# A 2-D FFT filter refactored: 32-point row DFT first, folded column DFTs, no spectrum transposes

## The chip, the cores and the metric

The kernel runs on one core of a Trainium2 chip. The metric is the device time of one execution in microseconds, as the median of several runs; lower is better. The profile's own clock (its "span") leaves out some 1.5 to 2 us at the ends. Engines are named as in the profile: PE is TensorE, PEld its weight load, DVE is VectorE, ACT is ScalarE, POOL is GpSimd, SP issues transfers. "Ratio" always means the mean time of one kernel's fast runs over the mean of the other's fast runs of the same rounds, so it is not quite the ratio of the medians quoted beside it.

## The reference, cut to what matters

```python
def reference(A_x, A_w_r, A_w_i, B_x, B_w_gate, B_w_up, B_w_down):
    xn = _layernorm(A_x, axis=-1)                       # [1, 2048, 640], bf16 in
    # filter: 2-D real FFT, product with a complex table, inverse
    X  = rfft2(xn.astype(float32), axes=(-2, -1)) * (A_w_r + 1j * A_w_i)
    a  = irfft2(X, s=(2048, 640), axes=(-2, -1)).astype(bfloat16)
    # gated bilinear unit, hidden size 1536
    b  = ((xn @ B_w_gate) * (xn @ B_w_up)) @ B_w_down
    return A_x + a + b                                  # bf16
```

(`rfft2` and `irfft2` are written in full in the reference; B_x is not used.) Both branches end up as matmuls: the transforms are products with tables of cosines and sines.

## The kernel before

A small scheduler inside the kernel plans every instruction at build time, from estimated durations, and fixes the order on each engine; on the chip each engine runs its list in that order and waits on semaphores. TensorE interleaves the filter's small matmuls with the gate and up projection ("GU", ten matmuls of 256 columns a tile, 96 tiles) and the down projection.

The filter before: each block of 128 rows is transposed, goes through the DFT over the 640 features (which has the even and odd features apart), is folded while it is read from PSUM, and goes through a 128-point DFT. Then the spectrum is transposed, goes through 16-point DFTs, is multiplied by the filter, and comes back the same way. Two parts:

```python
# fold of the feature DFT: each addition has one operand in PSUM (e3), one in SBUF (v_osb)
e3 = ps[:, bk, 0:324].rearrange("p (c l) -> p c l", c=2)
c.e.tensor_tensor(v_a[:, ar, :, 0:161], e3[:, :, 0:161], v_osb[:, ar, :, 0:161], AluOpType.add)
c.e.tensor_tensor(v_a[:, ar, 0, 320:160:-1], e3[:, 0, 0:160], v_osb[:, ar, 0, 0:160], AluOpType.subtract)
c.e.tensor_tensor(v_a[:, ar, 1, 320:160:-1], v_osb[:, ar, 1, 0:160], e3[:, 1, 0:160], AluOpType.subtract)
# ...
# layer norm of blocks 2 to 15: two passes on GpSimd, x - m and then * rs
c.e.tensor_scalar(v_xn[:, sl, :], v_x[:, slx, :], 1.0, v_nmbf[:, b:b + 1], AluOpType.mult, AluOpType.add)
c.e.tensor_scalar(v_xn[:, sl, :], v_xn[:, sl, :], v_rs[:, b:b + 1], 0.0, AluOpType.mult, AluOpType.add)
```

## Time and profile before

| | before |
|---|---|
| time, median of the first 3 runs | 239.8 us (239.51 to 242.7) |
| span of the profiled run | 238.3 us |
| TensorE busy | 232.5 us, 98% |
| VectorE busy | 173.8 us, 73% |
| GpSimd busy | 24.3 us, 10% |

The prediction below shows the lines on busy time, clock and chain. Three more views. First the slices of the page (40 equal slices of 6 us; each digit is the busy share in tenths):

```profile
PE   8979999999999999999999999999999999999995
...
DVE  5969998855479999999847422222278888888895
...
POOL 0027856800000000000000000000000000000000
```

TensorE shows 9 from the fourth slice to the last but one. GpSimd works in slices 3 to 8 only, about 12 to 48 us: that is the layer norm of the later blocks. Second, the lines of the page on GpSimd's two passes and on the largest fold (operands, count, then busy us and mean ns of one, then the idle time before them):

```profile
L797 POOL TENSOR_SCALAR arena<-arena 128x640 bf16<-128x640 bf16 x14 | 11.0, 798 | 17.0 <-DVE arena L742 14.9
...
L808 POOL TENSOR_SCALAR arena<-arena 128x640 bf16<-128x640 bf16 x14 | 11.1, 807 | 6.1 <-DVE arena L786 6.1
...
L865 DVE TENSOR_TENSOR arena<-ps,arena 128x322 bf16<-128x322 f32 x16 | 7.8, 488 | 3.6 <-ACT arena L856 3.5
```

A fold reads `ps,arena`: one operand from PSUM, one from SBUF (`ps` is the kernel's buffer in PSUM, which the matmuls write, `arena` its one large buffer in SBUF). Third, what TensorE waited for in the first 62 us (us in total, times, longest):

```profile
PE ps L879 <- DMA arena<-c_t: 1.8, 1, 1.8
PE ps L700 <- DVE arena L707: 1.1, 1, 1.1
```

### The profile page before, as it was taken

Reading aid. Unit: us, or ns where it says so; the run is one execution under the profiler, and the core shown is the slowest. Engines: PE = TensorE matmul, PEld = TensorE weight load, DVE = VectorE, ACT = ScalarE, POOL = GpSimd, SP = SyncE. Lnnn points to the kernel's source line nnn. Section 1 sums busy time; section 2 is a strip of 40 time slices with the busy share of each in tenths; the row PEclk is TensorE's granted clock in tenths of the full one; section 3 lists DMA queues with packets and bytes.
Section 4 is the critical chain, followed back from the end, with each engine's and each line's share of the span. In section 5 each row is a group of like instructions: output and inputs, shape, how many; then the busy total and the mean of one; then the engine's idle time right before and its main releaser. Section 6 shows DMA issues by size and latency. Waiting matters only on the chain.

```text
span 238.3 us, 5579 instructions
## 1 busy us (share of the span) xinstructions
PE 232.5 (98%) x2274; PEld 197.8 (83%) x2274; DVE 173.8 (73%) x502; ACT 108.9 (46%) x181; POOL 24.3 (10%) x35
## 2 busy tenths in 40 slices
PE   8979999999999999999999999999999999999995
PEld 8968888787999999998988888888787787787773
DVE  5969998855479999999847422222278888888895
ACT  2135667676554565554577555555223223223120
POOL 0027856800000000000000000000000000000000
PEclk9999999999999999999999999999999999999999
DMA  6999700960720000001072100000013223123221
GB/s 199 346 338 384 260 3 0 256 190 0 267 89 3 3 0 3 0 3 56 3 241 92 55 3 0 0 3 0 17 43 98 56 69 99 55 73 96 68 60 55
DMA packets 18953, 21.35 MB, mean 90 GB/s; under 512 B 1520, under 2 KB 17520, under 8 KB 18800
## 3 DMA queue, kind: packets, MB, share of 16 engines
q1 hardware_dynamic: 18928, 20.99, 27.7%
q8 instruction: 18, 0.29, 0.5%
q14 instruction: 7, 0.06, 0.1%
HBM read 18.37 MB, written 2.62 MB: 88 GB/s over the span
## 4 chain that ended last, share of the span: by engine, by line
PE 93%; SPq 3%; DMA 2%; DVE 1%; issue 0%; ACT 0%
PE ps L1064 44%; PE ps L1211 22%; PE ps L846 5%; SPq L666 3%; PE ps L1112 3%; DMA arena<-c_t 2%; PE ps L1159 2%; PE ps L977 2%; PE ps L1158 2%; PE ps L998 2%; PE ps L921 2%; PE ps L942 2%; PE ps L821 2%; PE ps L1122 2%; PE ps L879 1%; PE ps L880 1%
## 5 line engine op out<-in xcount | busy, mean ns | idle before, releaser
L1064 PE MATMUL ps<-arena 128*128 128x256 bf16 x960 | 110.5, 273 | 0.2 <-ACT arena L1075 0.2
L1064 PEld LDWEIGHTS ps<-arena 128*128 128x128 bf16 x960 | 92.9, 98 | 11.5 <-ACT arena L1075 0.4
L1075 ACT ACTIVATE arena<-ps 128x512 bf16<-128x512 f32 x96 | 57.3, 597 | 49.7 <-PE ps L1064 49.2
L1211 PE MATMUL ps<-arena 128*128 128x320 bf16 x384 | 54.6, 299 | 0.0
L1082 DVE TENSOR_TENSOR arena<-arena 128x256 bf16<-128x256 bf16 x93 | 26.6, 285 | 33.4 <-ACT arena L1075 33.2
L1211 PEld LDWEIGHTS ps<-arena 128*128 128x128 bf16 x384 | 37.5, 98 | 13.6
L1169 ACT ACTIVATE arena<-ps 128x644 f32<-128x644 f32 x16 | 11.2, 707 | 47.4 <-PE ps L1159 47.4
L956 DVE TENSOR_TENSOR arena<-ps,arena 128x512 bf16<-128x512 f32 (+1 forms) x44 | 25.3, 636 | 0.0
L1221 DVE TENSOR_TENSOR arena<-ps,arena 128x320 bf16<-128x320 f32 x32 | 15.6, 488 | 3.8 <-PE ps L1211 3.4
L846 PE MATMUL ps<-arena 128*128 128x324 bf16 x96 | 15.6, 300 | 0.0
L1009 ACT ACTIVATE arena<-ps 128x1024 bf16<-128x1024 f32 x10 | 10.2, 1022 | 8.8 <-PE ps L998 8.8
L891 ACT ACTIVATE arena<-ps 128x648 bf16<-128x648 f32 x16 | 11.4, 710 | 5.9 <-PE ps L882 5.5
L1199 DVE TENSOR_TENSOR arena<-arena 128x640 f32<-128x640 f32 x16 | 13.1, 818 | 0.4
L797 POOL TENSOR_SCALAR arena<-arena 128x640 bf16<-128x640 bf16 x14 | 11.0, 798 | 17.0 <-DVE arena L742 14.9
L1143 DVE CAST arena<-ps 68x256 bf16<-68x256 f32 x15 | 6.3, 420 | 8.6 <-PE ps L1122 8.6
L846 PEld LDWEIGHTS ps<-arena 128*128 128x128 bf16 x96 | 9.2, 97 | 3.6
L808 POOL TENSOR_SCALAR arena<-arena 128x640 bf16<-128x640 bf16 x14 | 11.1, 807 | 6.1 <-DVE arena L786 6.1
L1159 PE MATMUL ps<-arena 128*128 128x161 bf16 x64 | 10.7, 235 | 0.0
L1158 PE MATMUL ps<-arena 128*128 128x161 bf16 x64 | 10.6, 233 | 0.0
L865 DVE TENSOR_TENSOR arena<-ps,arena 128x322 bf16<-128x322 f32 x16 | 7.8, 488 | 3.6 <-ACT arena L856 3.5
L1132 ACT ACTIVATE arena<-ps 128x512 bf16<-128x512 f32 x16 | 9.5, 593 | 0.7 <-PE ps L1112 0.6
L989 DVE COPY arena<-ps 128x1024 bf16<-128x1024 bf16 (+1 forms) x11 | 7.1, 649 | 3.5 <-PE ps L977 3.5
(71 smaller groups left out, 259.1 us busy)
## 6 DMA issues: line engine op xcount, KB each, us to landing
arena<-in_A_x_dram SPq DMA_DIRECT2D x18, 160.0 KB, 2.2
out_dram<-arena SPq DMA_DIRECT2D x32, 80.0 KB, 1.6
arena<-c_tinv SPq DMA_DIRECT2D x1, 2048.0 KB, 8.2
arena<-in_B_w_gate_dram SPq DMA_DIRECT2D x15, 128.0 KB, 5.0
arena<-in_B_w_up_dram SPq DMA_DIRECT2D x15, 128.0 KB, 3.6
arena<-in_A_x_dram SPq DMA_DIRECT2D x3, 640.0 KB, 7.0
arena<-in_B_w_down_dram SPq DMA_DIRECT2D x1, 1920.0 KB, 8.1
arena<-c_t SPq DMA_DIRECT2D x4, 384.0 KB, 6.3
```

Of the source, the lines that this page charges most:

```text
L846: ins = c.e.matmul(ps[:, bk + q // 3, 0:324], v_xt[:, tj, b * 128:(b + 1) * 128], v_fd[:, q, :], start=(q % 3 == 0), stop=(q % 3 == 2))
L891: return c.e.activation(dst, src, _ACTF.Copy)
L956: ins = c.e.tensor_tensor(dst, x5[:, :, cc, :, :], wv, AluOpType.mult)
L1064: ins = c.e.matmul(ps[:, bk, w * 256:(w + 1) * 256], v_gw[:, w, j, r, :], v_xt[:, j, c8 * 256:(c8 + 1) * 256], start=(j == 0), stop=(j == 4))
L1075: return c.e.activation(v_gbf[:, rr, :], ps[:, bk, :], _ACTF.Copy)
L1082: return c.e.tensor_tensor(v_ht[:, ft, c8 * 256:(c8 + 1) * 256], v_gbf[:, rr, 0:256], v_gbf[:, rr, 256:512], AluOpType.mult)
L1158: c.e.matmul(dst, v_z2[:, r3, kt, cc, :], v_g[:, 2 * o4, :], start=True, stop=False)
L1159: ins = c.e.matmul(dst, v_z2[:, r3, 2, cc, :], v_g[:, 2 * o4 + 1, :], start=False, stop=True)
L1169: return c.e.activation(dst, src, _ACTF.Copy)
L1199: return c.e.tensor_tensor(v_yn[:, r2, :], v_yn[:, r2, :], v_xr[:, r2, :], AluOpType.add)
L1211: ins = c.e.matmul(ps[:, bk, 0:320], v_ht[:, ft, sa * 128:(sa + 1) * 128], v_wd[:, ft, hf * 320:(hf + 1) * 320], start=(ft == 0), stop=(ft ...
L1221: return c.e.tensor_tensor(v_out[:, r2, sl3], ps[:, bk, 0:320], v_yn[:, r2, sl3], AluOpType.add)
```

## The change

The intent is to take work off the engine that bounds the kernel. The row DFT comes first: a real 32-point DFT of four interleaved groups of rows is one 128x128 table, applied to each normalized block. The symmetry of the feature DFT is used before it (two levels of folding: 640 features become four groups of 160), so its matmuls shrink. The remaining 64-point row transform and the twiddle factors become one 128x128 complex table for each pair of frequencies, and the spectrum is never transposed. Removed: 4 x 81 small matmuls of 128 columns. Added: 80 for the row DFT, 32 at the end, and folds on VectorE whose operands are both in SBUF. The core of the diff, heavily cut:

```diff
-        b_a = alloc("A", 2 * 2 * _LP, at=o_bt)
...
+        v_l = V("L").bitcast(_F32).rearrange("p (r c d) -> p r c d", r=2, c=2)
+        v_f = V("F").rearrange("p (r d g) -> p r g d", r=3, g=4)      # group index innermost
...
-                def em_d(c, b=b):          # feature DFT of a block, then the fold from PSUM (above)
...
+                def em_l1(c, sl=sl, lr=lr):                           # first fold, both operands in SBUF
+                    x0 = v_xn[:, sl, 0:320]
+                    x1 = v_xn[:, sl, 639:319:-1]
+                    c.e.tensor_tensor(v_l[:, lr, 0, :], x0, x1, _OP.add)
+                    return c.e.tensor_tensor(v_l[:, lr, 1, :], x0, x1, _OP.subtract)
...
+                def em_l2(c, lr=lr, fr=fr):                           # second fold
+                    c0 = v_l[:, lr, :, 0:160]
+                    c1 = v_l[:, lr, :, 319:159:-1]
+                    c.e.tensor_tensor(v_f[:, fr, 0:4:3, :], c0, c1, _OP.add)
+                    return c.e.tensor_tensor(v_f[:, fr, 1:3, :], c0, c1, _OP.subtract)
...
+                def em_r(c, fr=fr):                                   # 32-point row DFT
+                        st = v_f[:, fr, j, 0:128] if j < 4 else v_ff[:, fr, 512:640]
+                        ins = c.e.matmul(psflat[:, ...], st, v_sm[:, 1, :], start=True, stop=True)
...
-            def em_t1(c, lb0=lb0, n=n):    # spectrum transpose (and em_t2, and both 16-point DFTs)
```

`v_f`: group index innermost. Four consecutive bf16 belong to four groups. The layout gives the row DFT four tidy chunks.

## The prediction

> **What bounds the kernel now.** I read the page first: busy time, slices, chain. The span is 238.3 us, the median time 239.8, so 1.5 us lies outside the span.
>
> ```profile
> PE 232.5 (98%) x2274; PEld 197.8 (83%) x2274; DVE 173.8 (73%) x502; ACT 108.9 (46%) x181; POOL 24.3 (10%) x35
> ...
> PEclk9999999999999999999999999999999999999999
> ...
> PE 93%; SPq 3%; DMA 2%; DVE 1%; issue 0%; ACT 0%
> ```
>
> TensorE is busy 98% at full clock and holds 93% of the chain that ended last. A busy matmul row is not yet a full array, so I looked for real idling in two more views. In the waits, TensorE's own total is 3.1 us, all but 0.2 of it at the start. In the chain in order of time, rows of equal matmuls give the rate:
>
> ```profile
> 15.56 2.18 PE ps L1064 x20
> ...
> 22.13 1.66 PE ps L846 x12
> ...
> 62.29 0.89 PE ps L921 x16
> ...
> 178.85 3.26 PE ps L1211 x24
> ```
>
> Dividing: 256 columns take 0.109 us (the gate/up projection, GU), 324 columns 0.138, 128 columns 0.056, 320 columns 0.136 (down projection). The timeline near 200 us shows the 161-column matmuls starting 0.07 apart. Summed: GU 960 x 0.109 = 104.8; down 384 x 0.136 = 52.2; row DFT 96 x 0.138 = 13.3; forward 128-point 64 x 0.138 = 8.8; inverse 128-point 96 x 0.109 = 10.5; final DFT 128 x 0.07 = 9.0; all transposes and 16-point DFTs (80 + 4 x 81) x 0.056 = 22.6. Total 221.2. The first packed work starts at 14.7 us and the tail after the last matmul is some 2.4; 14.7 + 221 - 2.4 (work done before 14.7) + 2.4 is 236, the span within 1%. So the kernel is bound by matmul columns streamed, from 14.7 us to the end; the other engines hide.
>
> **What the Trainium skill says.** "TensorE: Matmul & The Clock Gate", section "Back-to-back issue gap", gives N/2.4 + 2.5 ns for a warm matmul: 109.2 ns at 256 columns and 135.8 at 320. The trace agrees (0.109, 0.136). "VectorE: DVE Perf Modes", section "The perf-mode tier table", has tensor_tensor at one element per cycle for fp32, two for bf16 in SBUF. The trace agrees: 322 fp32 elements take 484 ns, 256 bf16 elements 285. Successive ones start closer: 0.40 and 0.20 us in the timeline, and I use these.
>
> "SBUF — State Buffer", section "Who interferes with whom", says that a VectorE instruction with two SBUF inputs contends with a GpSimd instruction that reads SBUF, by an exclusive lock held for the whole instruction. The trace shows it, in one place. L771 multiplies four elements from two SBUF operands:
>
> ```profile
> 34.55 0.80 POOL L797 TENSOR_SCALAR arena<-arena 128x640 bf16<-128x640 bf16 x1
> 34.71 0.64 DVE L771 TENSOR_TENSOR arena<-arena 128x4 f32<-128x4 bf16 x1
> ...
> 43.47 0.80 POOL L797 TENSOR_SCALAR arena<-arena 128x640 bf16<-128x640 bf16 x1
> 43.56 0.71 DVE L771 TENSOR_TENSOR arena<-arena 128x4 f32<-128x4 bf16 x1
> ...
> 16.94 0.15 DVE L771 TENSOR_TENSOR arena<-arena 128x2 f32<-128x2 bf16 x1
> ```
>
> Four elements took 0.64 and 0.71 us and ended within 0.01 us of the GpSimd instruction beside them; with GpSimd idle, 0.15. Before the change this costs little, as the row stage's folds (L865 to L868) take one input from PSUM.
>
> **The change part by part.** It removes both spectrum transposes and both 16-point DFTs (4 x 81 matmuls, -18.1 us of TensorE). The forward and inverse DFT over the feature axis shrink by folding: 13.3 to 32 x 0.136 + 64 x 0.069 = 8.8, and 9.0 to 8.8. It adds the 32-point row DFT (80 x 0.056 = 4.5) and 32 matmuls at the end of the down groups (32 x 0.136 = 4.4). The 128-point transforms keep their columns. Net -18.1 - 4.5 - 0.2 + 4.5 + 4.4 = -13.9: 207 us instead of 221. A 256-column GU can start at about 12.4 us (after the second block's layer norm, two folds and its evacuation on VectorE, from the same rows), not 14.7. Fully packed, 12.4 + 206.4 + 2.4 = 221 us of span, about **223 us** of time. That is the promise.
>
> The catch: every column transform now needs all 16 row blocks, and the final DFT all 16 spectrum tiles, so there are barriers. The instruction order gives four stages on TensorE:
> - Rows: 40 GU tiles, 160 small matmuls: 43.7 + 9.0 = 52.7.
> - Spectrum: 28.2 plus 14 GU tiles, 15.3: 43.5.
> - Final DFT: 8.8 plus 16 GU tiles and 4 down groups: 33.4.
> - Rest: 26 GU tiles, 28 down groups: 77.9.
>
> VectorE in the same stages, with start-to-start times of the trace. **Rows**: statistics 32 x 0.40 + 16 x 0.17 = 15.5; small layer-norm steps 2 x 1.9 + 4 x 1.4 = 9.4; new folds from SBUF 56 x 0.40 = 22.4; evacuation of all 16 transposes 16 x 0.42 = 6.7; products 28 x 0.20 = 5.6. Sum 59.6, from 2.95 us on: 62.6 at the earliest, against TensorE's 12.4 + 51.8 = 64.2. **Spectrum**: per tile two products of 644 from PSUM at 0.76 (L956 starts 0.62 apart for 512, of which 0.09 is fixed), two combinations at 0.40, an H: 2.57 x 16 = 41, against 43.5. **Final**: 64 x 0.42 + 16 x 0.20 + 4 x 0.40 = 32, against 33.4. So VectorE, 73% busy before, becomes level with TensorE in the first three stages: any wait of it is a wait of TensorE, as orders are fixed. In the second and third stage I add only the filling of the chain, 2.5 + 1.6.
>
> In the row stage the lock decides. GpSimd there: 28 layer-norm passes x 0.80, 8 folds x 0.83 (scaled from 667 ns for 256), 9 products x 0.67: 35 us, within some 60. VectorE has 84 instructions with two SBUF inputs in it (56 folds, 28 products) besides the L771 kind. Walking the order by layer-norm group, folds stand beside passes of GpSimd about half the time. I **choose** 30 of them blocked for 0.5 us (0.8 of a pass, of which some 0.2 at its ends lies outside the lock: the products at 28.18 and 47.28 us slipped in there). That is 15 us: the rows end near 62.6 + 15 = 78 instead of 64. Then 78 + 0.9 (last evacuation) + 46 + 35 + 77.9 + 2.4 = 240 us of span, 241.7 of time.
>
> Transfers: the filter now comes in 64 loads of 41 KB, four a tile, into four slots; 2 us to land (96 KB took 2.0) against 2.7 us of TensorE work a tile and three tiles of lead: hidden. The last gate/up load is issued only when its slots come free, some 6 us of TensorE work before its use, and 1.3 MB takes about that: up to 1 us.
>
> **The rivals.**
> 1. *The lock hardly bites.* For it: the products before the change, also with two SBUF inputs, show no blocked one (mean 285 ns). Then VectorE waits only for ACT and GpSimd results, 4 us or so: rows end at 67, span 229, time 231.
> 2. *The lock bites at its worst*: VectorE and GpSimd strictly alternate, 0.8 a turn. Then 45 blocked turns, 24 us: rows end at 87, span 249, time 250. Against it: the gaps just named.
> 3. *TensorE stays the bound throughout*, 223. Against it: VectorE's 59.6 us has no slack at all in the row stage.
> 4. *VectorE bounds the spectrum stage*, if the products with a stride of two run slower than 0.76: each 0.1 adds 3 us.
>
> **Range and chances.** I give my lock case three in four (241.7, with the blocked count 20 to 45: 236 to 249), the mild case one in four (231). The weighted middle is 239; I say **240**, range **230 to 249**. The 2% bounds are 235.0 and 244.6. Faster by over 2% needs the rows to end before 71: 0.32. Within 2%: 0.42. Slower: 0.26.
>
> **What the profile after would show.** TensorE busy falls by 14 us or more where idle time shows, to about 90% of the span, its idle time in the first 80 us and released by VectorE. The first D tile (new L942) starts at 78 if I am right, 65 to 67 if rival 1 is. Folds (L841 to L850) on VectorE average over 0.6 us if the lock bites, 0.48 if not; GpSimd passes over 0.85. The stage from the last down groups on is packed: 78 us. I am wrong if folds are at 0.48 and the rows yet end late (then a wait for ACT's square root, queued behind evacuations, holds the layer norm), or if the products of the spectrum stage exceed 0.9 us each.

## The result, and the profile after

The changed kernel took **255.21 us** (median of 4, 254.49 to 257.14) against 241.25 us of the kernel before in the same rounds (239.51 to 242.72). The ratio is 1.061, interval 1.052 to 1.069: slower, and above the predicted range.

Busy time, slices, granted clock and chain, from the page of the changed kernel (span 253.5 us, slices of 6.3 us):

```profile
PE 228.7 (90%) x2054; PEld 186.0 (73%) x2054; DVE 179.4 (71%) x420; ACT 98.9 (39%) x181; POOL 40.1 (16%) x49
...
PE   8997786696696999999899998999999999999985
...
DVE  5899999999989969999986998994322222222312
...
POOL 0018186177267200000000000000000000000000
PEclk9999999999999599999999999999999999999999
...
PE 54%; DVE 37%; DMA 3%; issue 2%; SPq 2%; ACT 1%; DVEq 0%
```

TensorE is no longer full in most of slices 4 to 13, and there VectorE shows 9 in all but one. The chain that TensorE had to 93% is now to 37% VectorE's. From slice 14 on TensorE is full again. So the loss is in the first stage, the row blocks. (The one 5 of `PEclk`, slice 14, is a stretch at half clock, from 81.9 to 88.8 us; experiment 2 comes back to it.) The table by stage (stretch, its length, then busy us of PE, PEld, DVE, ACT, POOL with instruction counts, granted clock, transfer share, GB/s), cut close to where the next stage starts:

```profile
12.40:90.80 78.40, 61.38 (x585) 49.55 (x583) 76.51 (x174) 32.75 (x57) 39.86 (x45) 0.96 0.26 90
90.80:136.50 45.70, 44.47 (x398) 36.50 (x397) 41.00 (x80) 31.58 (x61) 0.00 (x0) 1.00 0.26 52
136.50:171.50 35.00, 33.92 (x313) 28.61 (x312) 31.12 (x83) 16.66 (x33) 0.00 (x0) 1.00 0.37 115
171.50:253.50 82.00, 77.98 (x624) 60.53 (x622) 22.59 (x57) 15.52 (x26) 0.00 (x0) 0.99 0.18 52
```

In the row stage VectorE is busy 76.5 of 78.4 us, TensorE 61.4. The later stages have TensorE at 97%, 97% and 95%. What TensorE waits for most in the first 92 us, against the two waits of before:

```profile
PE ps L859 <- DVE arena L850: 10.5, 13, 2.0
PE ps L897 <- DVE arena L912: 3.2, 2, 1.9
PE ps L897 <- DVE arena L684: 1.4, 1, 1.4
```

L859 is the row DFT, L850 the second half of the second fold, L897 GU, L912 the product gate times up. The folds and GpSimd's second pass on the page:

```profile
L850 DVE TENSOR_TENSOR arena<-arena 128x320 bf16<-128x320 f32 x16 | 16.6, 1037 | 0.0
L849 DVE TENSOR_TENSOR arena<-arena 128x320 bf16<-128x320 f32 x16 | 15.6, 977 | 0.0
L809 POOL TENSOR_SCALAR arena<-arena 128x640 bf16<-128x640 bf16 x14 | 12.9, 931 | 2.2 <-DVE arena L788 1.8
...
L842 DVE TENSOR_TENSOR arena<-arena 128x320 f32<-128x320 bf16 x12 | 8.6, 720 | 0.0
```

The second folds (L849, L850) take about 1 us each, twice the 488 ns of the fold before with nearly as many elements. GpSimd's passes slowed too, from 807 to 931 ns.

A mean mixes cases, so I looked at single ones. The timeline of VectorE has a second fold with GpSimd still idle, and later one beside a pass of it (start, duration, instruction):

```profile
8.27 0.87 DVE L849 TENSOR_TENSOR arena<-arena 128x320 bf16<-128x320 f32 x1
8.94 0.91 DVE L850 TENSOR_TENSOR arena<-arena 128x320 bf16<-128x320 f32 x1
...
38.02 1.38 DVE L850 TENSOR_TENSOR arena<-arena 128x320 bf16<-128x320 f32 x1
```

and GpSimd and TensorE beside the last of these:

```profile
37.38 1.31 POOL L799 TENSOR_SCALAR arena<-arena 128x640 bf16<-128x640 bf16 x1
...
39.46 0.47 PE L859 MATMUL ps<-arena 128*128 128x128 bf16 x5 [1.48 <-DVE arena L850]
```

The fold starts at 38.02 under a pass that lasts until 38.69, and ends at 39.40; TensorE, idle for 1.48 us, starts 0.06 us later. That is the hold-up that was predicted. But the fold at 8.27 is followed 0.67 us later by the next, with no GpSimd work anywhere near. That cost was not predicted. So there were two suspects of different kinds.

From the trace I took the start-to-start time of each VectorE instruction in the row stage, less the idle time, and split it by whether a GpSimd instruction overlapped:

| VectorE instruction, row stage | GpSimd idle | GpSimd working |
|---|---|---|
| first fold (L841, L842) | 0.43 us | 0.77 us |
| second fold (L849, L850) | 0.71 us | 0.99 us |
| product (L912) | 0.21 us | 0.54 us |
| statistics (L727, L728) | 0.39 us | 0.39 us |
| evacuation from PSUM (L684) | 0.46 us (4 only) | 0.40 us |

The last two rows have one operand from SBUF or PSUM and do not notice GpSimd. In the kernel before, the folds with one operand in PSUM (L865) do not either: 0.41 us in the 8 cases with GpSimd idle, 0.40 in the 8 beside its work. The excess of the first three and of L773 over the left column, summed over the 48 blocked instructions, is about 15 us. The excess of the 32 second folds over 0.40 us is 10 us.

### The profile page after: what moved, and what is told of

Its sections match the earlier page's. It is cut to its first block, busy times and chain, and to the rows that moved or that the text cites. A ratio compares the mean times of both kernels' runs of the same rounds, so it can differ in the third digit from the quotient of the medians.

```text
span 253.5 us, 5073 instructions
## 1 busy us (share of the span) xinstructions
PE 228.7 (90%) x2054; PEld 186.0 (73%) x2054; DVE 179.4 (71%) x420; ACT 98.9 (39%) x181; POOL 40.1 (16%) x49
## 4 chain that ended last, share of the span: by engine, by line
PE 54%; DVE 37%; DMA 3%; issue 2%; SPq 2%; ACT 1%; DVEq 0%
PE ps L897 22%; PE ps L1085 21%; DVE arena L981 6%; DVE arena L912 5%; DVE arena L850 5%; DVE arena L849 4%; DMA arena<-in_B_w_up_dram 3%; DVE arena L842 3%; DVE arena L841 2%; PE ps L710 2%; DVE arena L684 2%; SPq L677 2%; DVE arena L728 2%; PE ps L1087 2%; DVE arena L991 2%
## 5 line engine op out<-in xcount | busy, mean ns | idle before, releaser
L683 ACT ACTIVATE arena<-ps 128x512 bf16<-128x512 f32 (+3 forms) x174 | 96.7, 582 | 140.0 <-PE ps L897 98.5
L897 PE MATMUL ps<-arena 128*128 128x256 bf16 x960 | 116.8, 276 | 6.8 <-DVE arena L912 3.2
L897 PEld LDWEIGHTS ps<-arena 128*128 128x128 bf16 x960 | 92.8, 99 | 21.0 <-DVE arena L912 4.3
L1085 PE MATMUL ps<-arena 128*128 128x320 bf16 x384 | 56.8, 299 | 1.1 <-DVE arena L912 1.1
L912 DVE TENSOR_TENSOR arena<-arena 128x256 bf16<-128x256 bf16 x87 | 30.5, 350 | 29.8 <-ACT arena L683 29.2
L981 DVE TENSOR_TENSOR arena<-ps,arena 128x644 f32<-128x644 f32 x32 | 24.9, 820 | 1.3 <-PE ps L970 1.3
L859 PE MATMUL ps<-arena 128*128 128x128 bf16 x80 | 8.0, 234 | 10.5 <-DVE arena L850 10.5
L850 DVE TENSOR_TENSOR arena<-arena 128x320 bf16<-128x320 f32 x16 | 16.6, 1037 | 0.0
L849 DVE TENSOR_TENSOR arena<-arena 128x320 bf16<-128x320 f32 x16 | 15.6, 977 | 0.0
L859 PEld LDWEIGHTS ps<-arena 128*128 128x128 bf16 x80 | 5.3, 116 | 13.9 <-DVE arena L850 11.8
L1000 PE MATMUL ps<-arena 128*128 128x256 bf16 x64 | 9.6, 272 | 0.6 <-ACT arena L683 0.6
L1087 PE MATMUL ps<-arena 128*128 128x320 bf16 x32 | 9.6, 299 | 0.0
L1044 PE MATMUL ps<-arena 128*128 128x160 bf16 x64 | 9.3, 231 | 0.0
L1040 PE MATMUL ps<-arena 66*128 66x320 bf16 x32 | 9.3, 300 | 0.0
L946 PE MATMUL ps<-arena 128*128 128x160 bf16 x64 | 9.1, 233 | 0.0
L942 PE MATMUL ps<-arena 128*128 128x320 bf16 x32 | 9.1, 299 | 0.0
L727 DVE BATCH_NORM_STATS2 arena<-arena 128x6 f32<-128x320 bf16 x16 | 7.4, 464 | 2.0 <-DMA arena<-in_A_x_dram 2.0
L842 DVE TENSOR_TENSOR arena<-arena 128x320 f32<-128x320 bf16 x12 | 8.6, 720 | 0.0
```

Source lines behind the costliest of these rows:

```text
L683: return c.e.activation(dst, src, _ACTF.Copy)
L842: return c.e.tensor_tensor(v_l[:, lr, 1, :], x0, x1, _OP.subtract)
L849: c.e.tensor_tensor(v_f[:, fr, 0:4:3, :], c0, c1, _OP.add)
L850: return c.e.tensor_tensor(v_f[:, fr, 1:3, :], c0, c1, _OP.subtract)
L859: ins = c.e.matmul(psflat[:, bk * 512 + j * 128: bk * 512 + (j + 1) * 128], st, v_sm[:, 1, :], start=True, stop=True)
L897: ins = c.e.matmul(ps[:, bk, w * 256:(w + 1) * 256], v_gw[:, w, j, r, :], v_xt[:, j, c8 * 256:(c8 + 1) * 256], start=(j == 0), stop=(j == 4))
```

## The experiments

The first theory, **A**: the row stage lasts as long as VectorE's queue; it is too long by 10 us for the 8-byte output step and by 15 us for GpSimd's passes. Rivals: **B**, the second fold is slow for another reason (reversed input, f32 input) or the row stage waits for something else; **C**, GpSimd's passes coincide with slow folds but do not cause them.

One number is used to compare runs: TensorE's **lost time** up to the first matmul of the spectrum stage. For each matmul I take the time to the next one's start, less the usual time for its number of columns (the 5th percentile in the same trace), and sum. It counts idle time and slow clock, and does not depend on how much work the plan put there.

**1. The step by itself.** The changed kernel with additions of 320 elements appended at its end, where GpSimd is idle.

```diff
+            for _ in range(3):
+                c.e.tensor_tensor(out_bf(4), a, b, _OP.add)     # output step 4 elements; others: 1, 2, 8, f32, bf16 inputs
...
```

> The changed kernel with 22 extra VectorE additions at its very end, GpSimd idle, to measure the second fold's cost by itself. Each reads two fp32 operands of 320 columns from SBUF, unless said otherwise. Theory A (the 8-byte step of the bf16 output costs): packed output 0.40 us start to start, reversed input with packed output 0.40, step of 4 bf16 elements 0.70. Rival B (the reversed fp32 input costs): reversed input with packed output 0.70, forward input with step 4 0.40. Steps of 2 and 8, an fp32 output with a step of 2, and bf16 inputs are measured to see where the cost starts. The outputs stay right, the time is some 10 us longer than the changed kernel's.

It took 266.8 us in one look, state unknown, with a correct result. The tail of VectorE's timeline (start, length of the group, count):

```profile
252.27 1.28 DVE L1120 TENSOR_TENSOR arena<-arena 128x320 bf16<-128x320 f32 x3
253.47 1.28 DVE L1122 TENSOR_TENSOR arena<-arena 128x320 bf16<-128x320 f32 x3
254.68 1.31 DVE L1124 TENSOR_TENSOR arena<-arena 128x320 bf16<-128x320 f32 x3
255.89 2.28 DVE L1126 TENSOR_TENSOR arena<-arena 128x320 bf16<-128x320 f32 x3
257.96 3.04 DVE L1128 TENSOR_TENSOR arena<-arena 128x320 bf16<-128x320 f32 x2
260.60 1.52 DVE L1130 TENSOR_TENSOR arena<-arena 128x320 f32<-128x320 f32 x3
262.04 0.79 DVE L1132 TENSOR_TENSOR arena<-arena 128x320 bf16<-128x320 bf16 x3
262.74 1.56 DVE L1134 TENSOR_TENSOR arena<-arena 128x320 bf16<-128x320 bf16 x2
```

Dividing the distance to the next group's start by the count: packed output 0.40 us; second input reversed 0.40; output step 2 elements (4 bytes) 0.40; step 4 (8 bytes) **0.69**; step 8 (16 bytes) 1.32; f32 output with a step of 8 bytes 0.48; all bf16, packed, with a reversed input 0.23; all bf16 with a step of 8 bytes 0.68 (the next instruction starts at 264.10). So the reversal costs nothing, and f32 inputs with a packed output take the 0.40 us that I had assumed; the 8-byte step of a bf16 output makes it 0.69, and it also takes away what all-bf16 operands would gain.

**2. The packed second fold.** Group index outermost; the table of the feature DFT, and the chunks that the row DFT reads, are rearranged to match. Every engine has its instructions in the order of the changed kernel.

```diff
-        v_f = V("F").rearrange("p (r d g) -> p r g d", r=3, g=4)
+        v_f = V("F").rearrange("p (r g d) -> p r g d", r=3, g=4)
...
-                        st = v_f[:, fr, j, 0:128] if j < 4 else v_ff[:, fr, 512:640]
+                        st = v_ff[:, fr, j * 128:(j + 1) * 128]
```

> The changed kernel with the second fold written packed (group by group) and the column table rearranged for it: same instructions in the same order, same columns on TensorE, only the output step of 32 VectorE instructions changes from 8 bytes to 2. Theory A (step): each falls from 0.70 to 0.40 us where GpSimd is idle, the row stage ends 10 us sooner (first column transform at 80 to 82 instead of 90.8), time 244 to 247. Rival B (reversed input, or the lock alone): no fold gets shorter, time stays at 254 to 256.

It took 245.2 us (243.85 to 245.89), correct, ratio to the kernel before 1.019 (1.012 to 1.025). The second folds fell from 977 and 1037 ns to these means, 0.40 us start to start with GpSimd idle:

```profile
L852 DVE TENSOR_TENSOR arena<-arena 128x320 bf16<-128x320 f32 x16 | 9.2, 577 | 0.0
...
L853 DVE TENSOR_TENSOR arena<-arena 128x320 bf16<-128x320 f32 x16 | 9.1, 567 | 0.0
```

Ten microseconds less on VectorE, ten less in all. The step is a cause, and B falls for it. Two other things changed with it. The weights of the 80 row-DFT matmuls are now read packed too: their loads fell from 116 to 97 ns, 1.5 us in sum on an engine that was waiting. And the half clock from 81.9 to 88.8 us is gone. VectorE was busy in all of 76 to 88 us of the changed kernel, so that clock did not hold the folds up; from the end of the last fold to the next stage it took 2.2 us there and 1.6 here, so the clock accounts for some 0.6 of the ten.

**3. Layer norm on ScalarE, no GpSimd work** (and, in a second kernel, the packed fold as well). One activation pass with scale and bias replaces both GpSimd passes; GpSimd's share of first folds and products goes to VectorE.

```diff
+                        return c.e.activation(v_xn[:, sl, :], v_x[:, b, :], _ACTF.Identity,
+                                              bias=v_nb[:, b:b + 1], scale=v_rs[:, b:b + 1])
...
-                T("L1_%d" % b, opts.get("l1_eng", ("dve", "pool")), ...
+                T("L1_%d" % b, opts.get("l1_eng", ("dve",)), ...
```

> The changed kernel with nothing left on GpSimd in the row stage: layer norm of blocks 2 to 15 as one ScalarE pass each (14 x 0.8 us), all folds and products on VectorE; the strided output is kept. Theory (lock): no fold and no product is longer than when alone (0.41, 0.70, 0.20), the 16 us of blocked time go, some 5 us of work come to VectorE in exchange: row stage ends near 80, time 243 to 247. Rival (the lock is not the cause of the long folds): folds stay at 0.7 to 1.0 and the time is 258 or more, as VectorE got more work.

> Both edits together. If the strided output and the lock are the two missing parts of the row stage and add up, VectorE needs 81 - 16 - 10 + 5 = 60 us there, rows end at 66 to 68, the time is 230 to 233: faster than the kernel before by 3 to 4%. If another cause holds the row stage (ScalarE's square roots queued behind evacuations, TensorE's clock dropping in its idle gaps), the row stage ends at 75 or later and the time is 240 or more.

Both missed: 253.9 us (253.45 to 258.19; the profile fell in a slow run) and 243.7 us (243.13 to 244.39). The folds were unblocked, as the theory wanted (first folds 0.42 us, second 0.69 or 0.40, products 0.21). Yet the gain over the changed and the packed kernel was 1.3 and 1.5 us. The trace shows why this says little about GpSimd: the scheduler, given other durations, made another plan. In the second of the two the row stage ended at 69.9 us, 11 sooner than in experiment 2, but with 300 GU matmuls in it instead of 400; 100 x 0.109 = 10.9 us of TensorE work had moved behind it. The lost time was 17.5 us, against 18.3. A stage that ends sooner with less in it is no gain. And VectorE took over GpSimd's folds and products.

**4. GpSimd's passes cut short, order kept.** To take away the hold-up and nothing else, the 28 passes cover 64 columns instead of 640. The result is wrong. All instructions on TensorE, VectorE and ScalarE stand in the order of the changed kernel.

```diff
+        T("xn_zero", "pool", 1500.0, lambda c: c.e.memset(v_xn[:, 2:8, :], 0.0), ...)
...
-                        return c.e.tensor_scalar(v_xn[:, sl, :], v_x[:, b, :], 1.0, v_nmbf[:, b:b + 1],
+                        return c.e.tensor_scalar(v_xn[:, sl, 0:64], v_x[:, b, 0:64], 1.0, v_nmbf[:, b:b + 1],
```

> The changed kernel, with GpSimd's 28 layer-norm passes shortened from 640 to 64 columns (the rest of their output is set to zero once at the start, so the result is wrong on purpose); the order of instructions on TensorE, VectorE and ScalarE is the same as in the changed kernel. Theory (GpSimd's passes hold up VectorE's additions and products that read two operands from SBUF, some 16 us in the row stage): the first folds fall to 0.42 us, the products to 0.21 us, the second folds stay at 0.70 us (their output step), the row stage ends 11 to 15 us sooner than the 90.8 us of the changed kernel, and the whole takes 241 to 245 us. Rival (the passes do not hold VectorE up, the additions are slow by themselves or the row stage waits for ScalarE): 252 us or more.

> The packed second fold and the shortened GpSimd passes together (wrong on purpose, same order of instructions as the changed kernel). If the two costs add, 255.2 - 10.0 - 12 = 233 us, range 230 to 236, with the row stage ending near 69 us. If VectorE is not what the row stage waits for once either is gone, no better than 241 us.

Alone it took 246.7 us (245.09 to 247.4), 8.5 less than the changed kernel; with the packed fold 236.7 us (235.83 to 237.12), 8.5 less than the packed kernel. The row stage ended at 84.1 and 73.1 us. Both just missed what was expected (241 to 245 and 230 to 236), as less came off. The second folds stayed at 0.71 us with GpSimd idle in the first kernel, so the two costs are separate, and they add: 10.0 and 8.5 alone, 18.5 together. C falls. Nor is it that the layer norm came sooner: VectorE's idle time in the row stage did not shrink (gaps of 2.6 us after 12.4 us in the changed kernel, 4.4 with short passes), its instructions did. The gain was smaller than the 11 to 15 us I expected, because GpSimd kept its folds and products: 22 of VectorE's folds still overlap them in the second kernel and show 0.3 us more each.

**5. Folds in bf16, planned anew.** The packed fold, no GpSimd work, the first fold's output in bf16, and the scheduler told the new durations; the layer norm once on ScalarE, once on VectorE.

```diff
-        v_l = V("L").bitcast(_F32).rearrange("p (r c d) -> p r c d", r=2, c=2)
+        v_l = V("L").rearrange("p (r c d) -> p r c d", r=2, c=2)
...
-                {"dve": 2 * (320 * 1.04 + 65), "pool": 1700.0},
+                {"dve": 2 * _d_dve_tt16(320), "pool": 1700.0},
```

> Packed second fold, layer norm of blocks 2 to 15 as one ScalarE pass, no GpSimd work, and the first fold's output kept in bf16 instead of f32, so that both folds have bf16 operands only (a correct kernel if the tolerance allows). Theory (in the earlier kernel with the first two of these, VectorE's queue still was full in the row stage: 62 us of work and gaps in 69.8 us): 64 additions of 0.40 us become 0.23 us, 11 us less on VectorE, and the whole takes 231 to 236 us. Rival (that kernel's row stage waits for ScalarE, whose layer-norm passes come in groups of four, 3.4 us, ahead of the PSUM evacuations): 240 us or more.

> As the one with the folds in bf16, but the one-pass layer norm of blocks 2 to 15 is on VectorE (14 passes of about 0.3 us, 4 us in sum) instead of ScalarE (14 passes of 0.84 us). Theory that VectorE's queue is what counts: 2 to 4 us slower than with ScalarE, 234 to 239 us. Rival that ScalarE's groups of passes ahead of the evacuations count: faster than with ScalarE, 228 to 233 us.

Both missed again, in the wrong direction: 246.7 us (245.61 to 247.93) and 251.1 us (250.43 to 252.25), both correct. Again the plan had changed: only 220 and 210 GU matmuls before the spectrum stage, and a lost time of 17.7 and 20.9 us in a row stage that ended at 61.7 and 64.7 us. In the first, VectorE was still busy 43.2 us of the 49.3 from 12.4 to 61.7 us, while the plan had only 220 x 0.109 + 160 x 0.056 = 33 us of work for TensorE there. So the shorter list left TensorE idle, as far as the trace shows. Which of the two, the shorter list or the place of the layer-norm groups in it, cost how much can't be told from these runs: both changed at once, and I leave it open. The lesson was to keep the order.

**6. One GpSimd pass instead of two, order kept; then the folds in bf16 as well.** The second pass does `(x - m) * rs` by itself; the first is cut to 2 columns, so that every list keeps its length and order. Both kernels are correct.

```diff
-                        return c.e.tensor_scalar(v_xn[:, sl, :], v_xn[:, sl, :], v_rs[:, b:b + 1], 0.0,
-                                                 _OP.mult, _OP.add)
+                        return c.e.tensor_scalar(v_xn[:, sl, :], v_x[:, b, :], v_nmbf[:, b:b + 1], v_rs[:, b:b + 1],
+                                                 _OP.add, _OP.mult)
```

> The packed second fold, and GpSimd's layer norm of blocks 2 to 15 in one pass over 640 columns, (x - m) * rs, in place of two (its other pass is cut to 2 columns so that every engine keeps the order of the changed kernel). Correct. Theory: about half of the blocked additions and products go; 28 shortened passes with the packed fold gave 236.7 us and none 245.2, so halfway, 240 to 242 us. Rival (GpSimd's time counts only while it exceeds some slack): within 1 us of 245.2 or of 236.7.

> As the one-pass kernel, with the first fold's output in bf16, so that both folds have bf16 operands alone and may run at 0.23 us instead of 0.40 where GpSimd leaves them alone; same order of instructions. Theory (VectorE's queue is the row stage's bound as long as TensorE idles there): 64 additions less 10 to 13 that GpSimd does, 0.17 us each, 8 to 9 us less on VectorE, 233 to 236 us, faster than the kernel before. Rival (GpSimd holds the bf16 folds up as long as the f32 ones): 238 to 241 us.

With the packed fold, one pass took 239.1 us (238.4 to 239.25), ratio 0.993 (0.989 to 0.996), a microsecond below what I expected. With bf16 folds on top it took **232.1 us** (231.26 to 233.46), ratio 0.965 (0.960 to 0.969), faster than the kernel before. That is a little under the 233 to 236 us expected. The rival, that GpSimd holds bf16 folds up as long, falls: 7 us came off. It still holds them up, though: 0.47 us beside GpSimd, 0.24 to 0.26 without. The row stage and the spectrum stage of this kernel (columns as in the table by stage above):

```profile
12.40:69.50 57.10, 54.89 (x575) 48.31 (x573) 52.18 (x172) 32.14 (x57) 30.77 (x45) 1.00 0.35 121
69.50:114.40 44.90, 44.30 (x398) 36.40 (x396) 40.76 (x80) 31.62 (x61) 0.00 (x0) 1.00 0.23 54
```

Nearly the same work as in the changed kernel's 78.4 us takes 57.1 here. TensorE is busy in 96% of it, at full clock; VectorE in 91%.

**7. A control: the same one-pass layer norm in the kernel before.** Same edit, same order.

> A control: the kernel before, with the same one-pass layer norm on GpSimd (its other pass cut to 2 columns; same order of instructions; correct). In the changed kernel with packed folds this was worth 6 us. Theory: GpSimd's time counts only where TensorE waits for VectorE; the kernel before has 3.8 us of lost TensorE time in its row stage and none of it is a wait for VectorE's folds, so within 1 us of it, 239 to 241 us. Rival (fewer GpSimd passes help any kernel): 236 us or less.

It took 240.12 us (239.33 to 240.51) against 240.13, ratio 0.998 (0.994 to 1.004). GpSimd's busy time fell from 24.3 to 17.8 us and nothing came of it: TensorE has no wait for VectorE's folds in that row stage.

All runs with the order of the changed kernel, side by side. In each, 400 GU matmuls stand ahead of the spectrum stage:

| kernel | time, us | spectrum stage starts | lost time till then |
|---|---|---|---|
| changed | 255.2 | 90.9 | 28.0 |
| packed fold | 245.2 | 81.2 | 18.3 |
| short passes (wrong result) | 246.7 | 84.1 | 21.3 |
| packed, short passes (wrong result) | 236.7 | 73.1 | 10.2 |
| packed, one pass | 239.1 | 75.9 | 13.0 |
| packed, one pass, bf16 folds | 232.1 | 69.5 | 6.6 |

From first to last row 21.4 us of lost time go, and 23.1 of time. (Up to 3.4 of the 28.0 and up to 1.7 of the 21.3 are stretches at half clock; the packed versions have none there.) The kernel before, with its own order, loses 3.8 us up to its spectrum stage.

## Why the prediction was wrong, point by point

- **What bounds the kernel before**: right. TensorE; the control (experiment 7) agrees.
- **TensorE's saving of 14 us**: right in size, as far as the traces show. By usual times per matmul, and without the warm-up and fill-in matmuls (166 x 0.056 = 9 us), the whole program sums to 206 us in the fastest version, against 220 in the kernel before. The changed kernel never got the saving, as TensorE waited instead.
- **VectorE becomes level with TensorE; its waits are TensorE's waits**: right. TensorE's waits in the row stage end with VectorE's folds and products.
- **The lock, 30 instructions x 0.5 = 15 us**: right in the sum, but by luck in its factors: 48 instructions, 0.3 us each, about 15 us. Experiment 4 shows that the passes cause at least 8.5 us of it; the rest (GpSimd's own folds and products) is read from the split table, not shown by a run.
- **The step that failed: "new folds from SBUF 56 x 0.40 = 22.4"**. I took 0.40 us from other additions of that size, all with packed outputs, and did not look at where the second fold writes. The 32 second folds cost 0.71 us with GpSimd idle, so the term was 22.4 + 32 x 0.31 = 32.3 us. Experiment 1 measured the cause, the 8-byte output step (0.69 against 0.40), experiment 2 took it away and got the 10 us back. This is the larger part of the miss.
- **No idle time of VectorE** in the row stage: 3 us of gaps were there. My terms gave 62.6 + 15 = 77.6 us for the end of the rows; 77.6 + 10 for the step + 3 for the gaps is 90.6, and the first tile of the next stage started at 90.9. The other terms (statistics, small layer-norm steps, products, evacuation, a memset that I had left out) cancel: the small layer-norm steps took 2 us less than my 9.4, the others differ by less than 1 us each.
- **The stages after**: right, within 2 us. Spectrum 45.7 us against 0.9 + 46 (VectorE's sum for a tile there was slightly off: its terms give 2.52 us, not 2.57); final DFT 35.0 against 35; rest 82.0 against 80.3. The product of rival 4 starts every 0.74 us, as assumed (0.76).
- **Rivals**: rival 2 named the end of rows at 87 and a time of 250, the nearest; but its mechanism, strict alternation with GpSimd, is not what happened: 45 blocked turns were to cost 24 us, 48 blocked instructions cost 15. The sign "I am wrong if folds are at 0.48 and the rows yet end late" did not come; the folds were slower than either case I had, and I had no case for a fold that is slow without GpSimd.

Where the expected gain went: off TensorE (14 us less to do), and given back as a new wait. The lost time rose by 28.0 - 3.8 = 24 us in the row stage, and by 4 us in the stages after (5.7 against 1.9: short waits for the chain to fill and for one load of the filter). 24 + 4 - 14 = 14 us, which is what the time rose by (255.2 - 241.25).

## What to carry to other kernels

When a change takes work from the engine that bounds a kernel and gives the next one its share, add up that next engine's queue in each stage, and price each new instruction by its operands' places and steps, not by its element count. A layout that is tidy for the reader can be dear for the writer: packing the output was worth 10 us here. And when a kernel plans itself, test one cost at a time with the order held fixed, since a new plan moves more than the edit; a stage that ends sooner proves nothing until one has counted what is in it.

## What the Trainium skill lacked or had wrong

- "SBUF — State Buffer", section "Door 1: The DMA port swizzle" (its note on cachelines), asks for two hits on a 16-byte line and puts the step that is free at 4 fp32 or 8 bf16. For VectorE's output it was not so: bf16 with a step of 8 bytes cost 0.69 us against 0.40 packed, f32 with the same step 0.48 (packed f32 additions of 322 elements, L1178 of the kernel before: 0.40), and bf16 with 16 bytes 1.32. A step of 4 bytes was free (0.40).
- "Vector Engine (DVE) Microarchitecture Reference", section 5.2, "Measured stream behaviour on trn2", does say that a destination whose elements are not adjacent slows the whole instruction (1.7 to 2.5 ns a column against 1.05), and would have warned me. It measured 4-byte words with long steps. Lacking are 2-byte outputs with short steps: here (0.69 - 0.40) / 320 = 0.9 ns more an element at 8 bytes, 2.9 at 16.
- "TensorE: Matmul & The Clock Gate", section "What's actually happening", has the clock fall after an idle window of about 3.4 us. In the kernel with bf16 folds and the layer norm on ScalarE it fell though no gap between matmuls in the row stage was longer than 2.5 us: granted clock 0.83 in the stretch from 30 to 40 us and 0.75 from 40 to 50, with TensorE busy 69% and 64%. The page's later section "A second HAM failure mode: psum-queue depth-cycling" does blame frequent short idles, but gives no figure. The traces give one: falls in one trace lie whole multiples of 3.41 us apart, and in the fast runs TensorE was busy 26 to 44% of the 3.41 us before each of the seven falls in the row stages. Stretches on the same grid that kept full clock had it busy 46% or more, from 8 us on. (The run of experiment 1 blurs this: 49% fell there and 45% did not.) No run set this share on purpose.
- "SBUF — State Buffer", section "Who interferes with whom", mentions a GpSimd measurement that was 1.5 times slower, but not for which instruction. Lacking is a figure for a stream of passes beside a busy VectorE: here the second pass of 128x640 bf16 took 931 ns on average in the changed kernel, 807 in the kernel before.
